# Weight tiles moved by 32 bytes, and products split at column 256 in place of 252

## The chip, the cores and the metric

The kernel runs on one core of a Trainium2 chip. The metric is the device time of the whole program in microseconds (us); smaller is better. Before the change the median of three runs is 719.89 us (717.8 to 721.41).

## What is computed

Two layers, each a linear-attention block followed by a mixture-of-experts block, on 2048 tokens of width 576, all in float32. Both layers use the same weights. Cut to what matters, one layer is:

```python
y = layernorm(x)
q, k, v = split(y @ wqkv)                      # 32 heads of 18
pq, pk = phi(q), phi(k)                        # phi(t) = where(t > 0, t + 1, exp(t)) + 1e-6
kv, z = sum_s pk^T v, sum_s pk                 # per head, over all tokens
x = x + (pq @ kv / (pq . z + 1e-6)) @ wo
y = layernorm(x)
s1, s2 = scores of y @ w_q against k1 and k2   # 32 heads, 8 + 8 sub-keys
e = argmax(s1) * 8 + argmax(s2)                # one expert of 64 for each head
x = x + sum_h gelu(y . u[e_h]) * v_expert[e_h]
```

## The kernel before, in words

**Tiling.** The 2048 tokens are 16 tiles of 128. For every tile and layer there are products with the weights: `front_k`, `front_v` and `front_q` (576 columns of output each), `back_out` (output of the attention, 576 columns), `exp_scores` (512 columns) and `exp_out` (expert results, 576 columns). In layer 1 the q products of tiles 0 to 12 are made late, by `late_q`.

**Precision.** A float32 product is made of float32r products (`F32R`): weights and tokens are each split in a high and a low part (`whi`, `wlo`; `thi`, `tlo`), and `passes` lists 14 products of 128 rows for the width of 576. `product` issues each of the 14 in two pieces, since one PSUM bank holds 512 columns: `PARTS` names for each piece its first and last column and where in the PSUM tile it goes. Each piece is one weight load on TensorE (the stationary operand, 128 x 128 of the tokens' transposed tile) and one matmul (the moving operand, 252 or 324 columns of a weight tile). A product is thus 28 matmuls, a scores product 14. `PARTS_V` places v differently: v is read back in groups of seven heads (126 columns), so its cut at 252 = 2 x 126 (`CUT`) has a reason. `row` gives the 576 columns of k, q, output and expert results as they lie in PSUM, across the boundary of two banks.

**Memory.** A pool gives out a partition's bytes in the order of declaration, each tile at a multiple of 32. As built, byte addresses within a partition and their remainders by 64:

| tile | use | before | remainder | after | remainder |
| --- | --- | --- | --- | --- | --- |
| `whi` | moving operand of k, q, v; stationary operand of `late_q` | 21,920 | 32 | 21,952 | 0 |
| `wlo`, `ohi`, `olo`, `shi`, `slo`, `vmix` | moving operands | 56,480 ... 125,600 | 32 | 56,512 ... 125,632 | 0 |
| `kvb` | plain float32 | 127,904 | 32 | 127,936 | 0 |
| `zb`, `junk`, `v5` | | 130,432 ... | 0 | 130,464 ... | 32 |
| `thif`, `tlof` and others of that pool | stationary operands | 181,504 ... | 0 | 181,536 ... | 32 |
| token tiles `x`, DMA targets and the rest of that pool | | 139,008 ... | mostly 0 | 139,040 ... | mostly 32 |

A row of `whi` is 3 x 576 x 4 = 6,912 bytes, 108 x 64, so all five blocks of a weight tile have the remainder of the tile; k and v begin 2,304 and 4,608 bytes on, multiples of 64 as well.

**Order.** On TensorE, VectorE (DVE), ScalarE (ACT) and GpSimd (POOL) the order of instructions is written out by hand (`play`, `in_order`). All DMAs are issued from SyncE's one queue (SP), in order, and SP is not among the engines whose order is fixed: there the framework's scheduler orders the issues. Some tiles are transposed by TensorE (`transposed`), others by `moved`: DVE transposes 32 x 32 blocks (`rf`, `rb`, `ro`), one DMA stores the result to DRAM (`y_df`, `y_db`, `y_do`), and four gather it back (`gf`, `gb`, `go`), after which ACT and DVE split it in `thi` and `tlo`. Names ending in f, b and o are of front, experts and output.

Of the kernel before, what the change touches and what calls it, by code (L numbers as in the profile page):

```python
# [11 lines left out]
F32 = mybir.dt.float32  # L12
# [9 lines left out]
S, D, H, DH = 2048, 576, 32, 18  # L22
P = 128
# [4 lines left out]
CUT = 2 * HC  # L28
# [36 lines left out]
def network(ctx, tc, x_in, wqkv, wo, wq_t, k_t, u_t, v2, c_mask, c_mask4, c_ident, c_code, c_code1, c_scale, c_shift, out):  # L65
    nc = tc.nc

    cp = ctx.enter_context(tc.tile_pool(name="cp", bufs=1))
# [8 lines left out]
        return t.rearrange("p (b c) -> p b c", b=2)[:, :, :HALF]  # L77

    def row(t):
        return t[:, 512 - CUT:512 - CUT + D]  # L80

    PARTS = (0, CUT, 512 - CUT), (CUT, D, 512)
    PARTS_V = (0, CUT, 0), (CUT, D, 512)


# [9 lines left out]
    nc.gpsimd.memset(mhalf, -0.5)  # L95
    kpad = cp.tile([P, 2, 56], F32, name="kpad")
    kraw = cp.tile([P, 2, E], F32, name="kraw")

    whi = cp.tile([P, NB, 3 * D], F32R, name="whi")
    wlo = cp.tile([P, 4, 3 * D], F32R, name="wlo")  # L100
# [151 lines left out]

    def product(tt, hi, lo, cols, n, parts=PARTS, rem=REM):

        o = psum(f"pp{n}")
        todo = passes(rem)
        for i, (a, b, w) in enumerate(todo):
            wb = hi[:, b] if w == "hi" else lo[:, blocks(rem)[b][1]]
            for c0, c1, at in parts:
                nc.tensor.matmul(o[:, at:at + c1 - c0], tt[a == "lo"][:, b, :], wb[:, cols + c0:cols + c1],  # L260
                                 start=(i == 0), stop=(i == len(todo) - 1))
        return o

    def pair_product(t0, t1, cols, n, parts=PARTS):

        o = [psum(f"pp{n}0_{t}") for t in (0, 1)]
        todo = sorted(passes(REM), key=lambda p: p[1])
        for i, (a, b, w) in enumerate(todo):
            wb = whi[:, b] if w == "hi" else wlo[:, blocks(REM)[b][1]]
            for p, tt in zip(o, (t0, t1)):  # L270
                for c0, c1, at in parts:
                    nc.tensor.matmul(p[:, at:at + c1 - c0], tt[a == "lo"][:, b, :], wb[:, cols + c0:cols + c1],  # L272
                                     start=(i == 0), stop=(i == len(todo) - 1))
        return o

    def phi(p, n):
        e = wk.tile([P, D], F32, tag="e", name=f"e{n}", bufs=4)
        nc.scalar.activation(e, row(p), AF.Exp)  # L278
        nc.vector.tensor_scalar(e, e, 1.0, EPS, op0=ALU.min, op1=ALU.add)  # L279
        nc.vector.scalar_tensor_tensor(e, row(p), 0.0, e, op0=ALU.max, op1=ALU.add)  # L280
        return e

    def phi_scalar(p, n):

        e = wk.tile([P, D], F32, tag="e", name=f"e{n}", bufs=4)
        nc.scalar.activation(e, row(p), AF.Relu, scale=-1.0)
        nc.scalar.activation(row(p), row(p), AF.Relu)
        nc.scalar.activation(e, e, AF.Exp, scale=-1.0)
        nc.vector.scalar_tensor_tensor(e, e, EPS, row(p), op0=ALU.add, op1=ALU.add)  # L289
        return e  # L290
# [18 lines left out]

    def front_pair(f, cols, parts=PARTS):  # L310
        pairs[f, 0, 0], pairs[f, 0, 1] = pair_product(tt["f", 0, 0], tt["f", 0, 1], cols, f, parts)
# [166 lines left out]
    def back_out(l, t):  # L478
# [4 lines left out]
        for i, (a, b, w, r) in enumerate(todo):  # L483
            for c0, c1, at in PARTS:
                nc.tensor.matmul(p[:, at:at + c1 - c0], hl[a][:r, b], w[:r, c0:c1], start=(i == 0), stop=(i == len(todo) - 1))  # L485
# [107 lines left out]
    def exp_base(l, t):  # L593

        p = tt["base", l, t] = psum(f"po{l}_{t}")
        x1 = xs.pop(("b", l, t))
        for c0, c1, at in PARTS:
            nc.tensor.matmul(p[:, at:at + c1 - c0], ident, x1[:, c0:c1], start=True, stop=False)

    def exp_out(l, t):  # L600
# [6 lines left out]
        for i in range(2):  # L607
            for c0, c1, at in PARTS:
                nc.tensor.matmul(p[:, at:at + c1 - c0], c[i], vmix[:, c0:c1], start=(i == 0 and not based), stop=(i == 1))  # L609
# [358 lines left out]
```

## Time and profile before

| | |
| --- | --- |
| median of the runs | 719.89 us |
| lowest and highest | 717.8 and 721.41 us |
| span of the profiled execution, first to last instruction | 717.5 us |
| mean granted TensorE clock | 0.996 |
| TensorE busy with matmuls | 699.1 us (97%) |
| VectorE busy | 469.5 us (65%) |
| ScalarE busy | 321.8 us (45%) |
| GpSimd busy | 202.6 us (28%) |

The profiled execution's own device time is not listed apart from its span. In the profile PE is TensorE's matmuls and PEld its weight loads. Matmuls are pipelined: the duration of one is longer than the time until the next one starts, so the rate of a stream is read from the difference of two starts. A timeline row has a group's start, the time from its first start to its last end, engine, line, operation, written tile <- read tiles, the shape of the first of them, and the count. Where an f32 matmul is not float32r (`F32`), one operation stands in the trace as two records.

### The profile page before, as it was taken

How to read it: one execution, taken by the hardware profiler on the slowest of the kernel's cores; microseconds unless marked ns; L12 is line 12 of the kernel's file. 1: busy time of each engine (PE TensorE's matmuls, PEld its weight loads, DVE VectorE, ACT ScalarE, POOL GpSimd, SP SyncE). 2: the span in 40 equal slices, each digit the busy share in tenths (PEclk: the TensorE clock that was granted, in tenths of full speed). 3: DMA queues.
4: the chain of work that ended last, by engine and by line, in shares of the span. 5: the costliest groups of instructions: out<-in, count | busy, mean ns of one | idle time of the engine just before them, and what ended most of it. 6: DMA issues, size and time to landing. Idle time of an engine off the chain costs nothing.

```text
span 717.5 us, 14670 instructions
## 1 busy us (share of the span) xinstructions
PE 699.1 (97%) x5464; PEld 650.5 (91%) x5464; DVE 469.5 (65%) x1005; ACT 321.8 (45%) x658; POOL 202.6 (28%) x544
## 2 busy tenths in 40 slices
PE   8999999999999999999999999999999999999995
PEld 5999989999998899899898989999899999999984
DVE  5533352435436877688777878552647788987986
ACT  4522332243224556455555655644543534444442
POOL 2210000111004533334344433210324244434441
PEclk9999999999999999999999999999999999999998
DMA  9947878775302322566777665513632324121101
GB/s 267 286 162 242 275 226 264 252 191 175 108 1 56 111 94 94 165 215 215 229 225 225 217 204 171 170 47 104 171 104 79 119 73 134 50 67 34 67 17 66
DMA packets 82711, 107.17 MB, mean 149 GB/s; under 512 B 8976, under 2 KB 47376, under 8 KB 82640
## 3 DMA queue, kind: packets, MB, share of 16 engines
q1 hardware_dynamic: 82640, 106.24, 47.4%
q8 instruction: 43, 0.70, 0.4%
q14 instruction: 28, 0.23, 0.1%
HBM read 68.88 MB, written 37.32 MB: 148 GB/s over the span
## 4 chain that ended last, share of the span: by engine, by line
PE 85%; DVE 5%; ACT 3%; DMA 3%; issue 2%; POOL 1%; SPq 0%; DVEq 0%; ACTq 0%; POOLq 0%
PE ppq L260 15%; PE ppo L485 15%; PE ppk L260 13%; PE ppv L260 12%; PE pps L527 10%; PE kva L527 4%; PE kva L362 2%; PE fold_ps L641 2%; PE ptb L217 2%; PE po L609 2%; DMA go<-y_do 2%; PE pto L217 2%; PE m L416 1%; PE ppk L272 1%; PE ppq L272 1%
## 5 line engine op out<-in xcount | busy, mean ns | idle before, releaser
L485 PE MATMUL ppo<-ohi,thio 126*128 126x252 f32 (+1 forms) x320 | 50.6, 300 | 4.5 <-ACT thio L119 4.4
L485 PEld LDWEIGHTS ppo<-ohi,thio 126*128 126x128 f32 (+1 forms) x320 | 44.9, 189 | 6.2 <-ACT thio L119 5.3
L260 PE MATMUL ppk<-whi,thif 128*128 128x252 f32 (+1 forms) x300 | 45.3, 298 | 0.8 <-ACT thif L119 0.8
L455 POOL TENSOR_TENSOR o<-pq,zb 128x576 f32<-128x576 f32 x19 | 27.4, 1443 | 62.5 <-ACT zb L401 58.7
L190 ACT ACTIVATE junk<-x,mb 128x576 bf16<-128x576 f32 x32 | 24.8, 775 | 44.6 <-POOL mb L189 44.4
L181 POOL TENSOR_SCALAR rsf<-mvf 128x1 f32<-128x1 f32 x16 | 3.4, 213 | 146.5 <-DVE mvf L178 146.4
L260 PE MATMUL ppv<-whi,thif 128*128 128x252 f32 (+1 forms) x300 | 44.6, 295 | 0.1
L260 PEld LDWEIGHTS ppk<-whi,thif 128*128 128x128 f32 x300 | 40.9, 188 | 4.0 <-issue 2.9
L207 ACT ACTIVATE yb<-x,rsb 128x640 f32<-128x640 f32 x32 | 29.5, 921 | 32.9 <-POOL rsb L197 32.9
L260 PE MATMUL ppv<-whi,tlof 128*128 128x252 f32 (+1 forms) x300 | 43.9, 293 | 0.0
L260 PE MATMUL ppk<-whi,tlof 128*128 128x252 f32 (+1 forms) x300 | 43.9, 293 | 0.0
L260 PEld LDWEIGHTS ppv<-whi,thif 128*128 128x128 f32 x300 | 41.3, 188 | 1.0 <-issue 0.4
L260 PEld LDWEIGHTS ppk<-whi,tlof 128*128 128x128 f32 x300 | 41.2, 188 | 0.0
L260 PEld LDWEIGHTS ppv<-whi,tlof 128*128 128x128 f32 x300 | 41.2, 188 | 0.0
L485 PE MATMUL ppo<-olo,thio 126*128 126x252 f32 (+1 forms) x256 | 39.5, 293 | 0.0
L260 PE MATMUL ppq<-whi 128*128 128x252 f32 (+1 forms) x260 | 39.5, 298 | 0.0
L485 PE MATMUL ppo<-ohi,tloo 126*128 126x252 f32 (+1 forms) x256 | 39.5, 293 | 0.0
L279 DVE TENSOR_SCALAR ek<-ek 128x576 f32<-128x576 f32 x16 | 7.3, 457 | 46.4 <-ACT ek L278 46.3
L260 PEld LDWEIGHTS ppq<-whi 128*128 128x128 f32 x260 | 36.0, 188 | 0.6 <-DVE eq L289 0.3
L485 PEld LDWEIGHTS ppo<-olo,thio 126*128 126x128 f32 x256 | 36.2, 188 | 0.0
L260 PE MATMUL ppk<-wlo,thif 128*128 128x252 f32 x240 | 36.1, 293 | 0.0
L260 PE MATMUL ppv<-wlo,thif 128*128 128x252 f32 x240 | 36.1, 293 | 0.0
(211 smaller groups left out, 1778.9 us busy)
## 6 DMA issues: line engine op xcount, KB each, us to landing
fold<-in_wq_t SPq DMA_DIRECT2D x64, 288.0 KB
whi<-hl_d SPq DMA_DIRECT2D x26, 320.0 KB
y_df<-rf SPq DMA_DIRECT2D x23, 320.0 KB
gf<-y_df SPq DMA_DIRECT2D x92, 80.0 KB
pq_d<-eq SPq DMA_DIRECT2D x19, 288.0 KB
pq<-pq_d SPq DMA_DIRECT2D x19, 288.0 KB
xf<-in_x SPq DMA_DIRECT2D x16, 288.0 KB
x<-in_x SPq DMA_DIRECT2D x16, 288.0 KB
```

What stands on the lines that cost most here:

```text
L190: nc.scalar.activation(junk, xt, AF.Square, bias=m[:, 0:1], accum_out=m[:, 1:2])
L207: nc.scalar.activation(y, x2, AF.Identity, scale=rs[:, 0:1], bias=rs[:, 1:2])
L217: nc.tensor.transpose(pt[:, b * P:(b + 1) * P], x, ident)
L260: nc.tensor.matmul(o[:, at:at + c1 - c0], tt[a == "lo"][:, b, :], wb[:, cols + c0:cols + c1], start=(i == 0), stop=(i == len(todo) - 1))
L272: nc.tensor.matmul(p[:, at:at + c1 - c0], tt[a == "lo"][:, b, :], wb[:, cols + c0:cols + c1], start=(i == 0), stop=(i == len(todo) - 1))
L279: nc.vector.tensor_scalar(e, e, 1.0, EPS, op0=ALU.min, op1=ALU.add)
L362: nc.tensor.matmul(a[64 * h:64 * h + 64, c * 72:c * 72 + n], vt[:, 2 * c + h], fk[:, f0:f0 + n], start=(t == 0 and c == 0), stop=(t == NT ...
L455: nc.gpsimd.tensor_tensor(o[:, :D], pq, zb, op=ALU.mult)
L485: nc.tensor.matmul(p[:, at:at + c1 - c0], hl[a][:r, b], w[:r, c0:c1], start=(i == 0), stop=(i == len(todo) - 1))
L527: nc.tensor.matmul(p[:, :512], hl[a == "lo"][:, b, :], shi[:, b] if w == "hi" else slo[:, blocks(REM)[b][1]], start=(i == 0), stop=(i == l ...
L609: nc.tensor.matmul(p[:, at:at + c1 - c0], c[i], vmix[:, c0:c1], start=(i == 0 and not based), stop=(i == 1))
L641: nc.tensor.matmul(p[32 * j:32 * j + 32, at:at + c1 - c0], kpad[:, ch // 2, 24 - 8 * a:56 - 8 * a], st[:, c0:c1], start=(a == 0), stop=(a ...
```

## The change

A tile `gap` of 32 bytes is declared ahead of `whi` and filled once by GpSimd, so that everything declared behind it moves up by 32 bytes. The two pieces of k, q, output and expert results become 256 and 320 columns in place of 252 and 324; they lie in PSUM at columns 256 and 512 of the tile, in place of 260 and 512. v keeps its cut at 252, the scores their single piece of 512.

```diff
     def row(t):
-        return t[:, 512 - CUT:512 - CUT + D]
-
-    PARTS = (0, CUT, 512 - CUT), (CUT, D, 512)
+        return t[:, 256:256 + D]
+
+    PARTS = (0, 256, 256), (256, D, 512)
     PARTS_V = (0, CUT, 0), (CUT, D, 512)
...
     kraw = cp.tile([P, 2, E], F32, name="kraw")
+    gap = cp.tile([P, 8], F32, name="gap")
+    nc.gpsimd.memset(gap, 0.0)
 
     whi = cp.tile([P, NB, 3 * D], F32R, name="whi")
```

TensorE, VectorE and ScalarE have the same instructions in the same order as before, GpSimd the one fill more. The scheduler orders SP's issues anew, though. Line numbers behind the gap are higher by two. The stretch of SP's queue around the gathers of tile 11 in the steady part of layer 0, before the change (`y_db0_11` is stored, its four gathers `gb0_11` follow, then `y_df1_9`, stored for tile 9 of layer 1, and its gathers):

```order
L233 DMA y_db0_11_5245<-rb0_11_5243 128x640
L617 DMA x_d9_147<-x20_9_5249 128x576
L239 DMA gb0_11_5349<-y_db0_11_5245 32x4x160 x4
L233 DMA y_df1_9_5358<-rf1_9_5356 128x640
L239 DMA gf1_9_5385<-y_df1_9_5358 32x4x160 x4
```

And after it:

```order
L235 DMA y_db0_11_5247<-rb0_11_5245 128x640
L619 DMA x_d9_149<-x20_9_5251 128x576
L235 DMA y_df1_9_5360<-rf1_9_5358 128x640
L241 DMA gb0_11_5351<-y_db0_11_5247 32x4x160 x4
L241 DMA gf1_9_5387<-y_df1_9_5360 32x4x160 x4
```

The store of `y_df1_9` went ahead of the four gathers of `gb0_11`; the same happens at tiles 7, 9 and 13. Earlier in the queue, near the end of layer 0's front, before the change:

```order
L707 DMA vst_2114<-in_v 64x576
L708 DMA vst_2114<-in_v 64x576
L712 DMA ust_2117<-in_u_t 128x64 x2
L714 DMA ust_2117<-in_u_t 64x64
L715 DMA ust_2117<-in_u_t 64x64
L712 DMA ust_2117<-in_u_t 128x64
L677 DMA xf_15_2088<-in_x 128x576
L233 DMA y_df0_11_1959<-rf0_11_1957 128x640
```

And after it:

```order
L679 DMA xf_15_2090<-in_x 128x576
L235 DMA y_df0_11_1961<-rf0_11_1959 128x640
L709 DMA vst_2116<-in_v 64x576
L710 DMA vst_2116<-in_v 64x576
L241 DMA gf0_11_2077<-y_df0_11_1961 32x4x160 x4
L714 DMA ust_2119<-in_u_t 128x64 x2
```

Here the load of token tile 15 and the store and gathers of tile 11 went ahead of the loads for the experts (`vst`, `ust`).

## The prediction

> **What bounds the kernel now.** I read the page's shares first, then the table by stage (windows), then the chain of waits, and last the timeline of TensorE. The page's first and fourth parts:
>
> ```profile
> PE 699.1 (97%) x5464; PEld 650.5 (91%) x5464; DVE 469.5 (65%) x1005; ACT 321.8 (45%) x658; POOL 202.6 (28%) x544
> ...
> PE 85%; DVE 5%; ACT 3%; DMA 3%; issue 2%; POOL 1%; SPq 0%; DVEq 0%; ACTq 0%; POOLq 0%
> ```
>
> A busy PE row need not be a PE at its peak, so the stages decide. Columns: window, its length, busy time of PE, weight loads, DVE, ACT, POOL, granted clock, DMA share, GB/s.
>
> ```profile
> 30.00:210.00 180.00, 180.00 (x1691) 169.69 (x1690) 73.77 (x148) 54.44 (x126) 13.58 (x39) 1.00 0.63 198
> 300.00:440.00 140.00, 134.90 (x1038) 126.94 (x1037) 114.23 (x244) 79.78 (x166) 54.90 (x145) 1.00 0.67 211
> 560.00:640.00 80.00, 79.98 (x547) 75.17 (x546) 68.65 (x154) 35.97 (x70) 33.74 (x93) 1.00 0.28 89
> 640.00:700.00 60.00, 59.98 (x393) 55.06 (x391) 53.06 (x126) 30.16 (x58) 24.28 (x67) 1.00 0.12 40
> ```
>
> From 30 to 210 us PE never stops and nothing else comes near it: a nanosecond off a matmul there is one off the span. Between 300 and 440 us PE loses 5 us to waits, and from 560 us on DVE is 86 to 88% busy, so a faster PE would soon wait for it. The granted clock is 1.00 throughout: nothing is to be had from the clock.
>
> How fast does the matmul stream run? The timeline merges neighbours, and the difference of two starts is the time of the group between them. Here are one `k` product, and one scores product between two others:
>
> ```profile
> 331.13 1.46 PE L260 MATMUL ppk<-whi,thif 128*128 128x252 f32 x10
> 332.43 1.20 PE L260 MATMUL ppk<-wlo,thif 128*128 128x252 f32 x8
> 333.47 1.46 PE L260 MATMUL ppk<-whi,tlof 128*128 128x252 f32 x10
> 334.77 1.50 PE L485 MATMUL ppo<-ohi,thio 126*128 126x252 f32 x10
> ...
> 339.74 1.10 PE L527 MATMUL kva<-slo,thib 128*128 128x512 f32 x4
> 340.67 1.33 PE L527 MATMUL kva<-shi,tlob 128*128 128x512 f32 x5
> ```
>
> Ten matmuls, five pairs of 252 + 324 columns, take 332.43 - 331.13 = 1.30 us: 260 ns a pair, 0.451 ns a column. The scores take 0.93 / 4 = 232.5 ns for 512 columns, 0.454 ns. What could a column cost? The durations of single matmuls by shape:
>
> ```profile
> L260 PE MATMUL ppk<-whi,tlof 128*128 128x324 f32 x150 | 40.5, 308 | 0.0
> L260 PE MATMUL ppk<-whi,tlof 128*128 128x252 f32 x150 | 39.5, 278 | 0.0
> L598 PE MATMUL po<-x,ident 128*128 128x324 f32 x6 | 2.1, 436 | 0.0
> L598 PE MATMUL po<-x,ident 128*128 128x252 f32 x6 | 1.8, 375 | 0.0
> ```
>
> 72 columns more cost 308 - 278 = 30 ns, 0.417 ns each. The plain-float32 matmul of L598 streams at half this rate (two cycles a column): 61 ns for 72 columns, 0.42 ns a cycle. So 576 columns could be streamed in about 576 x 0.42 = 242 ns, and 512 in 215; the kernel takes 260 and 232.5. **About 7% of the float32r stream is lost at something periodic**: 18 ns in 576 columns are 43 cycles, some 36 of which are 1 in 16 columns, that is, one for every 64 bytes.
>
> **The change, part by part.** As built, `whi` starts at byte 21,920 of a partition, which is 32 past a multiple of 64, and every weight tile behind it has the same remainder; the second piece starts 1,008 bytes on, at remainder 16. No float32r moving operand starts at a multiple of 64 today. Afterwards `whi` is at 21,952 (remainder 0) and a piece at 1,024 bytes on as well: all moving operands of k, q, output, scores and expert results are at 0. Of v only the first piece is; its second stays at remainder 48.
>
> *Moving operands.* The trace has no aligned float32r stream, so the price is bounded: nothing, if the lost cycle belongs to reading 4 bytes a cycle wherever one starts, and the whole loss if it comes from 64-byte reads that straddle two 64-byte rows. What the whole loss is worth: k, q and output make 32 products each of 14 pairs, expert results 64 pairs, together 1,408 pairs x 18 ns = 25.3 us. Of v, 448 pairs gain on the first piece alone, 18 x 252/576 = 8 ns: 3.6 us. Scores: 448 x (232.5 - 215) = 7.8 us. **Together 36.7 us.** I take the upper end as the likelier, because alignment at this grain is visible in one place, the next term. The columns stay 576 in both splits, so 256 + 320 in itself costs and saves nothing.
>
> *Stationary operands.* The gap of 32 bytes pushes everything behind the weights too, and `kvb` (2,528 bytes, 39.5 x 64) flips the remainder once more: the transposed tiles that are loaded as stationary operand go from remainder 0 to 32. The late q products of layer 1 take theirs out of `whi`, at remainder 32, today. Pieces of the chain, start and length in us:
>
> ```profile
> 42.91 3.64 PE ppq L260 x28
> ...
> 541.50 3.69 PE ppq L260 x28
> ```
>
> The first is a layer-0 product (stationary at 0), the second a late one (at 32): 0.05 us more for 28 matmuls. If this is due to the remainder, 115 products go over to it: 115 x 0.05 = 5.8 us; the 13 late ones get 0.65 back. Bounds 0 and 6; I take 5 with the gain, since both fit one cause.
>
> *SP's queue.* PE, DVE, ACT and POOL keep their order, and POOL gets one fill of 128x8 as one of its first instructions, while the first input is still on its way; it hides there, and uncovered would cost at most what a larger one does:
>
> ```profile
> 337.42 0.16 POOL L530 MEMSET s<- 128x64 f32 x1
> ```
>
> SP's order is set by a scheduler and changes: four times (gb of tiles 7, 9, 11, 13) the store `y_df` goes ahead of four gathers `gb` that stood before it. Timeline, tile 11:
>
> ```profile
> 395.93 2.59 SPq L239 DMA_DIRECT2D gb<-y_db  x4
> 399.32 0.34 SPq L233 DMA_DIRECT2D y_df<-rf  x1
> 401.51 1.76 SPq L239 DMA_DIRECT2D gf<-y_df  x4
> ...
> 398.45 0.83 DVE L231 STREAM_TRANSPOSE rf<-yf 128x640 f32<-128x640 f32 x1
> ...
> 402.00 0.73 ACT L119 ACTIVATE thib<-gb 128x640 fp32r<-128x640 f32 x1
> ...
> 403.84 1.42 PE L527 MATMUL kva<-shi,thib 128*128 128x512 f32 x5
> ```
>
> The store waits for `rf`, ready at 399.28; the gathers then leave at 399.7 instead of 395.93, 3.8 us later, the last at about 401.8. The store leaves at 399.32 and the first gather that reads it at 401.51, so a transfer lands some 2.2 us after its issue: the split `thib` starts near 404.0 instead of 402.00, ends at 404.7, and scores that began at 403.84 wait 0.9 us. Tiles 7, 9 and 13 by the same reckoning:
>
> ```profile
> 331.92 1.74 SPq L239 DMA_DIRECT2D gb<-y_db  x4
> 333.95 0.34 SPq L233 DMA_DIRECT2D y_df<-rf  x1
> ...
> 336.65 0.73 ACT L119 ACTIVATE thib<-gb 128x640 fp32r<-128x640 f32 x1
> ...
> 338.49 1.41 PE L527 MATMUL kva<-shi,thib 128*128 128x512 f32 x5
> ...
> 365.22 1.75 SPq L239 DMA_DIRECT2D gb<-y_db  x4
> 367.06 0.38 SPq L233 DMA_DIRECT2D y_df<-rf  x1
> 369.45 0.73 ACT L119 ACTIVATE thib<-gb 128x640 fp32r<-128x640 f32 x1
> 371.29 0.95 PE L527 MATMUL kva<-shi,thib 128*128 128x512 f32 x3
> ...
> 428.55 2.49 SPq L239 DMA_DIRECT2D gb<-y_db  x4
> 431.92 0.34 SPq L233 DMA_DIRECT2D y_df<-rf  x1
> ```
>
> Their gathers leave at 334.3, 367.5 and 432.3: 2.4, 2.3 and 3.7 us later. Tile 7 then lands near 337.8 and its scores wait about 0.15 us; tile 9 near 370.9, and they wait 0.4; tile 13 has some 2 us to spare. All four: 0.9 + 0.4 + 0.15, say 1.5 us. Bounds: 0, and the sum of the delays, 12.2 us. The loads of `ust` slip too, by up to 10 us near 150 us, and have time:
>
> ```profile
> 211.24 0.45 ACT L731 ACTIVATE shi<-ust 128x320 fp32r<-128x320 f32 x1
> ```
>
> *What is given back.* In the windows from 300 to 440 and 560 to 700 us, 280 of 717 us, PE is near other limits. If PE work falls 5%, DVE's 88% there becomes 93%, and the gathers between 300 and 440 us do not get faster. Least is lost if everything on the chain that is PE (85%, of 97% that PE is busy) follows: 12%, 4.4 us; most if those windows follow by nothing, 280/717 or 39%, 14.3 us. I take a quarter, 9 us.
>
> **Sum** against the profiled span: 36.7 - 9 - 5 - 1.5 = 21 us; 717.5 - 21 = 696.5. The median of the runs, 719.89, lies 2.4 us above the span, so **699 us**.
>
> **Rivals.**
>
> *A: the loss is in the rate, not in the address.* For it: 252 columns at remainder 32 and 324 at remainder 16 lose the same per column, and the L598 rows, with the 252 at remainder 0 and the 324 at 48, give 0.42 ns a cycle across both, so at half rate the address is nothing. Also the change moves moving and stationary operands together: they stay 32 bytes apart as before, and if only their distance counts, nothing happens. Against it: the late q rows. Then SP's 1.5 us remain: 721 us, 717 to 723. The Trainium skill, page "SBUF — State Buffer", section "Specifications (TRN2)", speaks for this rival: it gives lines of 16 bytes, with a penalty at each crossing to a new one; remainders 32 and 16 start on such a line already, so by that rule nothing is gained. The trace here fits as well a grain of 64.
>
> *B: slower.* The moving stream gains nothing, but the stationary loads at remainder 32 now cost in 115 products what they cost in the 13 late ones: +5.8 - 0.65, and scores pay about half of a pair's 3.6 ns each, 448 x 1.8 = 0.8 us. Place: every TensorE stage; it decides as soon as the moving gain is under 7.5 us. 719.9 + 6 + 1.5 = 727 us, 724 to 729. For it speaks the only row that has a stationary operand at 32; against it, that these also lie in the weight tile itself, so the cause may be another.
>
> *C: half.* Only the piece that starts on its tile's own boundary gains, or DVE takes back half: 36.7/2 - 6.5 = 12 us: 708 us, 705 to 714.
>
> For the floor, the Trainium skill, page "TensorE: Matmul & The Clock Gate", section "Back-to-back issue gap", gives N/2.4 + 2.5 ns: 245 ns a pair by estimate, against 260 measured; the sum by it would be some 4 us smaller. The sum above goes by the rows.
>
> **How the numbers follow.** Forecast 0.44 (691 to 705 by itself: 4.4 us given back and half the stationary price, 28 us; 15 us given back and all of it, 15 us), C 0.07, A 0.28, B 0.21. A measurement of this kernel tells about 0.5% from no change: 716.3 to 723.5. Faster: forecast and C, 0.51. Same: nearly all of A, 0.27. Slower: B and A's tail, 0.22. The range has to hold both signs: from 691, below which a sixth of the forecast's chance lies, to 726, above which half of B lies: 691 to 726.
>
> **What would show it.** Right: products of x28 near 3.45 us in the chain for k, q and output, v near 3.53, scores under 222 ns; PE's busy time down by 25 us or more, and more idle time of PE ahead of the scores and output between 300 and 440 us. Rival A: x28 still at 3.64 and late q too. Rival B: 3.69 everywhere, except the late q at 3.64. The SP step is wrong if `thib<-gb` waits for no DMA longer than now. The forecast falls with the first product between 30 and 210 us: there is nothing else that could shorten that stage.

## The result

The changed kernel takes 724.23 us (median of four runs, 723.09 to 724.62) against 718.85 us of the kernel before beside it. The ratio is 1.0074, with a 95% interval of 1.0045 to 1.0103: slower by 5.4 us, where 699 us was forecast. The profiled execution has a span of 722.7 us (717.5 before), at a mean granted clock of 0.996 as before.

The page of the changed kernel, its first and fourth parts:

```profile
PE 704.2 (97%) x5464; PEld 655.0 (91%) x5464; DVE 467.3 (65%) x1005; ACT 321.7 (45%) x658; POOL 201.9 (28%) x545
...
PE 73%; DVE 8%; DMA 6%; ACT 5%; issue 3%; SPq 3%; POOL 2%; DVEq 0%; ACTq 0%; POOLq 0%
```

PE is busy 5.1 us longer with the same 5464 matmuls over the same columns. The chain goes less over PE (73%, 85% before) and more over SP's queue, DMA and DVE: somewhere a wait has come in that was not there. The table by stage of the changed kernel says where (window, its length, busy time of PE, weight loads, DVE, ACT, POOL, granted clock, DMA share, GB/s):

```profile
30.00:210.00 180.00, 178.05 (x1664) 167.74 (x1663) 71.38 (x141) 53.70 (x125) 13.51 (x39) 1.00 0.63 200
300.00:440.00 140.00, 136.76 (x1049) 128.82 (x1049) 114.03 (x245) 78.16 (x163) 54.45 (x144) 1.00 0.69 213
```

Between 30 and 210 us, where PE never stopped before, it now stops for 1.95 us, and gets through 27 matmuls fewer (1664 in place of 1691). Between 300 and 440 us it waits less than before, 3.2 us in place of 5.1; 0.5 us of this is only that the last of these waits now falls behind 440 us, and up to 445 us it is 3.7 us in place of 5.1.

The streams themselves, from the timeline of the changed kernel: a piece of a `k` product and the start behind it, and a piece of a scores product and the start behind it.

```profile
337.30 1.48 PE L262 MATMUL ppk<-whi,tlof 128*128 128x256 f32 x10
338.62 1.49 PE L487 MATMUL ppo<-ohi,thio 126*128 126x256 f32 x10
...
343.85 1.10 PE L529 MATMUL kva<-slo,thib 128*128 128x512 f32 x4
344.79 1.33 PE L529 MATMUL kva<-shi,tlob 128*128 128x512 f32 x5
```

Five pairs of 256 + 320 columns take 1.32 us, 264 ns a pair, against 260 ns for 252 + 324 before. Four scores matmuls take 0.94 us, 235 ns each, against 232.5: no column has become cheaper. Whole products, from the chains: first a v product of the kernel before, then of the changed kernel a v product, a q product of layer 0 and a late q product of layer 1.

```profile
39.27 3.64 PE ppv L260 x28
...
39.32 3.64 PE ppv L262 x28
42.96 3.69 PE ppq L262 x28
...
545.89 3.73 PE ppq L262 x28
```

The v product kept its cut at 252, got an aligned first piece, and takes the 3.64 us it took before. The q product was cut anew and went from 3.64 to 3.69 us. The late q product went from 3.69 to 3.73.

### The profile page after: what moved, and what is told of

Its sections match the earlier page's. It is cut to its first block, busy times and chain, and to the rows that moved or that the text cites. A ratio compares the mean times of both kernels' runs of the same rounds, so it can differ in the third digit from the quotient of the medians.

```text
span 722.7 us, 14663 instructions
## 1 busy us (share of the span) xinstructions
PE 704.2 (97%) x5464; PEld 655.0 (91%) x5464; DVE 467.3 (65%) x1005; ACT 321.7 (45%) x658; POOL 201.9 (28%) x545
## 4 chain that ended last, share of the span: by engine, by line
PE 73%; DVE 8%; DMA 6%; ACT 5%; issue 3%; SPq 3%; POOL 2%; DVEq 0%; ACTq 0%; POOLq 0%
PE ppq L262 14%; PE ppo L487 13%; PE ppk L262 11%; PE ppv L262 10%; PE pps L529 10%; PE ptb L219 2%; PE fold_ps L643 2%; PE kva L364 2%; PE kva L529 2%; PE po L611 2%; SPq L241 2%; PE pto L219 2%; PE m L418 1%; DMA y_df<-rf 1%; DMA go<-y_do 1%
## 5 line engine op out<-in xcount | busy, mean ns | idle before, releaser
L487 PE MATMUL ppo<-ohi,thio 126*128 126x256 f32 (+1 forms) x320 | 50.6, 300 | 2.9 <-ACT thio L121 2.9
L262 PE MATMUL ppk<-whi,thif 128*128 128x256 f32 (+1 forms) x300 | 45.9, 299 | 0.8 <-ACT thif L121 0.8
L262 PE MATMUL ppk<-whi,tlof 128*128 128x256 f32 (+1 forms) x300 | 44.3, 294 | 0.0
L487 PE MATMUL ppo<-olo,thio 126*128 126x256 f32 (+1 forms) x256 | 40.1, 295 | 0.0
L487 PE MATMUL ppo<-ohi,tloo 126*128 126x256 f32 (+1 forms) x256 | 40.0, 295 | 0.0
L262 PE MATMUL ppq<-whi 128*128 128x256 f32 (+1 forms) x260 | 39.9, 300 | 0.0
L487 PEld LDWEIGHTS ppo<-olo,thio 126*128 126x128 f32 x256 | 36.7, 189 | 0.0
L487 PEld LDWEIGHTS ppo<-ohi,tloo 126*128 126x128 f32 x256 | 36.5, 189 | 0.0
L262 PE MATMUL ppk<-wlo,thif 128*128 128x256 f32 x240 | 36.5, 294 | 0.0
```

## The experiments

Two theories stood at the start. **Theory 1: the split costs.** The address of the moving operand is worth nothing, and 256 + 320 columns take longer than 252 + 324; what SyncE's new order adds is small. **Theory 2: the addresses cost**, be it the stationary operand at remainder 32 (rival B of the prediction) or another effect of the gap, which hides a gain of the moving operand. Later a third question came in: what SyncE's order costs by itself.

The runs that were timed against the kernel before, which took 718 to 719 us beside them:

| kernel | pieces | gap | order of SyncE | median, us | ratio, 95% interval | profiled span, us |
| --- | --- | --- | --- | --- | --- | --- |
| the change | 256 + 320 | yes | new | 724.23 | 1.0074, 1.0045 to 1.0103 | 722.7 |
| gap alone | 252 + 324 | yes | as before | 718.31 | 0.9991, 0.9977 to 1.0004 | 717.3 |
| split alone | 256 + 320 | no | new | 724.64 | 1.0084, 1.0064 to 1.0104 | 722.9 |
| order alone | 252 + 324 | no | new | 721.35 | 1.0040, 1.0023 to 1.0057 | 718.3 |
| change, old order | 256 + 320 | yes | as before | 722.47 | 1.0058, 1.0043 to 1.0073 | 720.7 |
| distance 96 | 252 + 324 | no | as before | 724.37 | 1.0081, 1.0059 to 1.0103 | 722.0 |
| scores at distance 0 | 252 + 324 | no | as before | 717.15 | 0.9986, 0.9971 to 1.0002 | 715.8 |
| split at 248 | 248 + 328 | no | as before | 722.29 | 1.0053, 1.0033 to 1.0072 | 721.0 |

### Streams of TensorE alone, by address and by size

A kernel of its own in place of the network: float32r matmuls one behind the other, 56 for each case, with start addresses and piece sizes chosen.

```diff
+    def group(name, pieces, mv, st, n=28, where=None, step=1728):
+        p = ps.tile([P, 1024], F32, tag="ps", name=name)
+        t = high if where is None else where
+        for i in range(n):
+            b = i % NB
+            w = t[:, st + b * P:st + b * P + P]
+            for c0, c, at in pieces:
+                m = low[:, mv + b * step + c0:mv + b * step + c0 + c]
+                nc.tensor.matmul(p[:, at:at + c], w, m, start=(i == 0), stop=(i == n - 1))
```

> No network here: TensorE alone streams groups of 28 pairs of float32r matmuls, with the split, the start addresses of both operands, the place in PSUM and the place of the stationary operand varied, and nothing else running; the output is a copy of the input. Theory now (the sizes of the two pieces decide, addresses do nothing): 252 + 324 takes 260 ns a pair at every start address, 256 + 320 about 264 at every start address, wherever the pieces go in PSUM. Rival (start addresses decide): the pairs change by 3 ns or more between moving operand at remainder 32 and 0 with one split. Rival (stationary address): they change between stationary at 0 and 32. If the stationary operand's place next to the moving one is what the late q products pay for, the two groups with it there take 3 ns more a pair than the same split with it far off. If the loss is 1 in 16 columns whatever the sizes, all other splits take 260 as well.

Measured, from the timeline of this kernel. The names say the split (`old` 252 + 324, `new` 256 + 320), and the remainder of moving (`mv`) and stationary (`st`) operand in units of 16 bytes (`two` is 32); `stlow` has its stationary operand in the moving operand's own tile, both at the same remainder.

```profile
23.11 7.45 PE L42 MATMUL oldxmvtwoxstzero<-low,high 128*128 128x252 f32 x56
30.40 7.54 PE L42 MATMUL oldxmvzeroxstzero<-low,high 128*128 128x252 f32 x56
37.78 7.63 PE L42 MATMUL oldxmvzeroxsttwo<-low,high 128*128 128x252 f32 x56
45.25 7.46 PE L42 MATMUL oldxmvbothxaligned<-low,high 128*128 128x252 f32 x56
52.55 7.50 PE L42 MATMUL newxmvtwoxstzero<-low,high 128*128 128x256 f32 x56
59.89 7.63 PE L42 MATMUL newxmvzeroxstzero<-low,high 128*128 128x256 f32 x56
67.35 7.67 PE L42 MATMUL newxmvzeroxsttwo<-low,high 128*128 128x256 f32 x56
...
96.93 7.55 PE L42 MATMUL oldxstlow<-low 128*128 128x252 f32 x56
104.31 7.62 PE L42 MATMUL newxstlow<-low 128*128 128x256 f32 x56
```

Two neighbouring starts divided by 28 give a pair, with the change from one case to the next in it: (30.40 - 23.11) / 28 = 260.4 ns for the split and the remainders of the kernel before, (37.78 - 30.40) / 28 = 263.6 with the moving operand moved to remainder 0. Within a case, without its first and last pairs, the values are 260.0 and 263.5 ns. The aligned stream is the slower one, and the expectation of one rate at every address has failed. With the stationary operand moved to 32 instead, the pair takes (45.25 - 37.78) / 28 = 266.8 ns. With both pieces started at a multiple of 64 it is 260.2: aligning gains nothing in any form. For 256 + 320 they are 262.4 (moving at 32, stationary at 0), 266.8 (both at 0) and 268.2 (moving at 0, stationary at 32). The split costs 2.4 ns a pair at the old remainders. Where in PSUM the pieces lie makes 1 ns or less.

The last two rows answer the late q products. Their 3.69 us do not come from a remainder of 32, but from the two operands being at the same remainder: 263.6 ns for 252 + 324. So what counts looks like the distance of the two, as rival A of the prediction had said in passing.

### The gap alone

```diff
     kraw = cp.tile([P, 2, E], F32, name="kraw")
+    gap = cp.tile([P, 8], F32, name="gap")
+    nc.gpsimd.memset(gap, 0.0)
```

> The 32 bytes alone, split kept at 252; SP's order is that of before. Sizes decide: ratio 1.000 (within 0.003), k products of 28 matmuls at 3.64 us. Addresses decide: about 1.007 as with the whole change.

Measured: ratio 0.9991 (0.9977 to 1.0004), no difference. The chain of this kernel, a q and a late q product:

```profile
42.77 3.64 PE ppq L262 x28
...
541.44 3.70 PE ppq L262 x28
```

They are the rows of before. Here the first pieces of k, q, output and expert results and all scores start at remainder 0 (the second pieces, 1,008 bytes on, at 48) and all stationary tiles at 32: the addresses of the change, without its sizes, are worth nothing in either direction. A gain of the moving operand hidden by a loss of the stationary one would show in the late q product, whose two operands both came from 32 to 0; it stayed at 3.70 us. Theory 2 falls, and with it the forecast's moving term and rival B's stationary one.

### The split alone

```diff
-        return t[:, 512 - CUT:512 - CUT + D]
-
-    PARTS = (0, CUT, 512 - CUT), (CUT, D, 512)
+        return t[:, 256:256 + D]
+
+    PARTS = (0, 256, 256), (256, D, 512)
```

> The split at 256 alone, no gap; SP's order is that of the whole change. Sizes decide (or SP's new order): ratio 1.007, k products of 28 matmuls near 3.69 us. Addresses decide: 1.000 and 3.64 us.

Measured: 1.0084 (1.0064 to 1.0104), span 722.9 us: the whole loss of the change, without the gap. Both pieces start at remainder 32 here and at 0 in the change, and the time is the same: this is the test of full alignment at these sizes, and it too finds nothing. The order of SyncE's issues is the changed kernel's too. So it is the sizes of the matmuls, not the addresses, that made the scheduler order the loads anew.

The trace of this run has one thing that the others lack (a stretch with its granted clock, third number from the end, and two rows of its timeline):

```profile
176.00:179.00 3.00, 3.00 (x23) 2.93 (x21) 1.63 (x4) 0.00 (x0) 0.92 (x3) 0.50 0.79 238
...
176.63 2.73 PE L260 MATMUL ppk<-whi,thif 128*128 128x256 f32 x10
179.18 1.22 PE L260 MATMUL ppk<-wlo,thif 128*128 128x256 f32 x8
```

The granted clock is 0.50 from 176 to 179 us, right behind a wait of TensorE of 2.03 us, and the ten `ppk` matmuls take 2.55 us in place of the changed kernel's 1.42. In the changed kernel, with a wait as long (1.95 us), the clock stayed at 1.00 there, so it is not shown that the wait brings this on; in this execution it made the loss over 1 us larger.

### What counts of an address

The distance of the moving operand's start from the stationary one's, in steps of 8 bytes, again in streams alone:

```diff
+    for r in range(0, 32, 2):                 # 4 bytes each: distance 0, 8, 16 ... 120
+        group("old" + L[r], split(252), r, 0, 20)
+    for r in range(0, 32, 2):
+        group("full" + L[r], [(0, 512, 0)], r, 0, 24)
...
+    group("oldstat", split(252), 0, 24, 20)
+    group("oldfar", split(252), 8 + 32, 0, 20)
+    group("oldfarther", split(252), 8 + 64, 0, 20)
```

> Streams alone again, 20 pairs each, nothing else running, the output a copy of the input. Now the stationary operand stays at a multiple of 128 bytes and the moving operand's start goes from 0 to 124 bytes past one, for 252 + 324, 248 + 328, 256 + 320, 288 + 288 and 512 columns. Theory (what counts is the distance between the two starts, modulo 128, together with the sizes): 252 + 324 takes 260 ns at distance 32, 263.5 at 0; the group with the stationary operand at 96 and the moving one at 0 (distance 32) takes 260 too, and so do those 128 and 256 bytes further; 512 columns take 233 at 32 and 227 at 0. Rival (the distance counts modulo 64): distance 96 takes 260 like 32. If some distance brings a pair under 257 ns, there is a version faster than both kernels; if the rate only steps between 260 and 267, the kernel before stands at the best point already.

Measured, 252 + 324 at distances 0, 8, 16, 24, 32 and 40 bytes (20 pairs each; timeline of this kernel):

```profile
23.09 5.45 PE L42 MATMUL olda<-low,high 128*128 128x252 f32 x40
28.38 5.58 PE L42 MATMUL oldc<-low,high 128*128 128x252 f32 x40
33.80 5.36 PE L42 MATMUL olde<-low,high 128*128 128x252 f32 x40
39.00 5.49 PE L42 MATMUL oldg<-low,high 128*128 128x252 f32 x40
44.33 5.37 PE L42 MATMUL oldi<-low,high 128*128 128x252 f32 x40
49.54 5.56 PE L42 MATMUL oldk<-low,high 128*128 128x252 f32 x40
```

Starts apart by 5.29, 5.42, 5.20, 5.33 and 5.21 us; within a case 263.9, 272.0, 260.0, 266.8, 259.9 and 270.1 ns a pair. Moving the stationary operand by 96 in place of the moving one by 32 gives 260.3, and distances of 160 and 288 bytes give 260.0: the distance counts modulo 128. The distance alone does not settle every value, though: 96 gave 264.5 ns here, by the moving operand, and 266.8 above, by the stationary one. The whole sweep for 252 + 324 runs from 259.9 to 272.0. The distances that are multiples of 16 average 263.3, those between them 268.6. The Trainium skill, page "SBUF — State Buffer", section "Specifications (TRN2)", has lines of 16 bytes with a penalty at each crossing to a new one. The sweep agrees with that grain, at some 5 ns a pair, and the kernel is on it before and after.

The kernel before, at distance 32, stands at the lowest of the sampled values. 256 + 320 is at 262.2 there and at 263.4 to 267.1 elsewhere, 248 + 328 at 260.2. So the old cut sits on a good point by its size, too, and both tiles move by 32 together in the change, which leaves the distance where it was.

### The distance changed in the kernel

`kpad` (448 bytes) is declared behind the weights in place of ahead of them, which puts the moving operands at distance 96; the sizes stay 252 + 324.

```diff
-    kpad = cp.tile([P, 2, 56], F32, name="kpad")
     kraw = cp.tile([P, 2, E], F32, name="kraw")
...
     vmix = cp.tile([P, D], F32R, name="vmix")
+    kpad = cp.tile([P, 2, 56], F32, name="kpad")
```

> Split at 252, SP's order of before; the tile kpad (64 bytes modulo 128) is declared behind the weights, so that every weight tile starts 96 bytes past a multiple of 128 and the transposed tiles stay at 0. Theory (the distance between the two starts modulo 128 counts): 264.5 ns a pair as in the streams, 4.5 ns x 1,674 pairs = 7.5 us more, scores and late q as before: ratio 1.010, k products of 28 matmuls near 3.70 us. Rival (in the kernel only the sizes matter): 1.000 and 3.64 us.

Measured: 1.0081 (1.0059 to 1.0103). From the chain of this kernel, a q and a late q product:

```profile
42.98 3.73 PE ppq L260 x28
...
546.05 3.69 PE ppq L260 x28
```

3.73 us where the distance changed, v included, and 3.69 as ever where it did not, since moving and stationary operand of a late q product lie in one tile. That the distance counts is thereby shown in the kernel itself, for these products. The size was near: the pair takes 266.7 ns where 264.5 was expected, and summed over the trace k, v, q and output take 8.6 us more where 7.5 was expected. The run takes 6.2 us more; between 300 and 440 us TensorE waits 2.7 us in place of 5.1, which is 2.4 us of the difference.

### The scores at distance 0

The one place where the streams promised a gain: 512 columns took 227.0 ns at distance 0 and 233.4 at 32. `vmix` and `kvb` are declared ahead of the scores' weights, and the late q's stationary blocks start 96 bytes later.

```diff
+    vmix = cp.tile([P, D], F32R, name="vmix")
+    kvb = cp.tile([P, 4 * HC + P], F32, name="kvb")
     shi = cp.tile([P, NB, 512], F32R, name="shi")
     slo = cp.tile([P, 4, 512], F32R, name="slo")
...
-        at = (1 + t // 2 % 2) * D + t % 2 * 2 * P
+        at = (1 + t // 2 % 2) * D + t % 2 * 2 * P + 24
```

> The kernel before with its tiles declared in another order, so that the scores' weights start at a multiple of 128 (distance 0 from the transposed tiles, where the stream of 512 columns took 227 ns in place of 233), all other weights staying at distance 32; and the late q products read their stationary operand 96 bytes further on (distance 32 in place of 0). Theory: 448 x 6.4 ns = 2.9 us and 182 x 3.3 ns = 0.6 us less, ratio 0.995. If the gain is eaten by waits elsewhere: 0.998 to 1.000.

Measured: 0.9986 (0.9971 to 1.0002), which cannot be told from no change. All scores together take 0.7 us less (232.2 ns a matmul, 233.8 before), not the 6.4 ns each that the streams promised; the late q products fall from 263 to 260 ns a pair, 0.4 us in all. For the scores, then, the stream alone does not carry over to the kernel. No version was found that is measurably faster than the kernel before.

### Another size: 248 + 328

```diff
-    PARTS = (0, CUT, 512 - CUT), (CUT, D, 512)
+    PARTS = (0, 248, 264), (248, D, 512)
```

> k, q, output and expert results split at 248 (248 + 328 columns), nothing else; SP's order of before. Theory (each size has its own rate at a given distance): 260.2 ns a pair in the streams at distance 32, so ratio 1.000, k products at 3.64 us. Rival (any split other than 252 costs): 1.007.

Measured: 1.0053 (1.0033 to 1.0072), and 264.5 ns a pair, where the streams alone had 260.2. A miss: the stream alone does not carry over to the kernel for this size either. SyncE's order is that of before here, so not every new size changes it. Whether the place in a sequence decides was tried with products of 14 pairs behind different work:

```diff
+        for r in range(5):                      # one behind the other
+            one(who + "same" + L[r], c)
+        for r in range(5):                      # behind a v product
+            one(who + "vee" + L[r], 252, at=0)
+            one(who + "turn" + L[r], c)
+        for r in range(5):                      # behind five matmuls of 128 columns
+            group(who + "few" + L[r], [(0, 128, 0)], 8, 0, 5)
+            one(who + "small" + L[r], c)
...
```

> TensorE streams alone again (the output is a copy of the input; the network is left out), all with moving operands at remainder 32 and stationary ones at 0: products of 14 pairs of 252 + 324, 248 + 328 and 256 + 320 columns as one stream of 70 pairs, one behind the other, behind a v product (252 + 324 written from column 0), behind five matmuls of 128 columns, and behind 14 of 512. Read: ns per pair within a product. Theory (a stream settles into one of several patterns by what stood before it, and keeps it): 248 + 328 takes 260 in the long stream and 264 to 265 behind v products or small matmuls, as it did in the whole kernel; 256 + 320 takes 262 to 263 in the long stream and 263 to 265 behind others; 252 + 324 takes 260 wherever it stands. Rival (what stands before does not matter, and the other engines' traffic makes the difference in the whole kernel): the same value in all five places, 260 for 248 + 328, 262.5 for 256 + 320, within 0.5 ns.

Measured, from the timeline of this kernel: two products one behind the other, of 252 + 324 (`old`), 248 + 328 (`two`) and 256 + 320 (`new`).

```profile
41.40 3.80 PE L42 MATMUL oldsamea<-low,high 128*128 128x252 f32 x28
45.04 3.80 PE L42 MATMUL oldsameb<-low,high 128*128 128x252 f32 x28
...
169.80 3.80 PE L42 MATMUL twosamea<-low,high 128*128 128x248 f32 x28
173.44 3.80 PE L42 MATMUL twosameb<-low,high 128*128 128x248 f32 x28
...
298.66 3.85 PE L42 MATMUL newsamea<-low,high 128*128 128x256 f32 x28
302.35 3.85 PE L42 MATMUL newsameb<-low,high 128*128 128x256 f32 x28
```

3.64, 3.64 and 3.69 us a product: 260.0, 260.0 and 263.6 ns a pair. 252 + 324 and 248 + 328 are at 260.0 in every place, after at most four uneven pairs. 256 + 320 has two patterns: pairs of 266 and 261 in turn (263.3 on average) in the long stream and behind its own kind, and 265, 265, 257 (262.4) behind v products and small matmuls, kept to the end of the product; behind 14 matmuls of 512 columns it falls into either. So for 256 + 320 there are several patterns, as the theory says, but with the values the other way round: the slower one was expected behind other work. For 248 + 328 the theory fails. The latter takes 267, 263 and 264 ns in turn in the kernel, as regularly, for a cause that stays open; the rival, traffic of other engines, was not tried.

### The order of SyncE's issues alone

The kernel before, with its 498 issues on SyncE pinned in the order that the changed kernel has:

```diff
+    SP_ORDER = [
+        0, 1, 2, 3, 4, 5, 6, 7, 8, 9, 10, 11, 12, 13, 14, 15, 16, 17, 18, 19, 20, 21, 22, 23,
...
+    for x, y in zip(SP_ORDER, SP_ORDER[1:]):
+        tc.add_manual_dep(dm[y], dm[x].name, mybir.DependencyInfo(mybir.DependencyClass.NoSync, mybir.DependencyReason.DATA),
+                          reason="in_order")
```

> The kernel before, with SP's 498 issues held in the order that they have in the changed kernel. If SP's new order does the harm: ratio 1.007. My step in the prediction: 1.5 us, ratio 1.002, scores of tile 11 about 0.9 us late. Theory now (the matmul stream alone sets the time): within 0.002 of 1.000.

Measured: 1.0040 (1.0023 to 1.0057), 2.9 us: more than either 0 or the prediction's 1.5 us, and less than the whole loss. First the timeline of the kernel before around the first attention; in brackets stands what an instruction waited for:

```profile
159.87 0.38 SPq L233 DMA_DIRECT2D y_df<-rf  x1
165.09 0.85 DVE L231 STREAM_TRANSPOSE rf<-yf 128x640 f32<-128x640 f32 x1 [0.34 <-DMA y_df<-rf]
168.34 0.92 ACT L207 ACTIVATE yf<-xf,rsf 128x640 f32<-128x640 f32 x1 [3.19 <-POOL rsf L183]
170.39 0.76 DVE L280 SCALAR_TENSOR_TENSOR ek<-ppk,ek 128x576 f32<-128x576 f32 x1
171.55 1.43 PE L362 MATMUL kva<-ek,v 128*64 128x72 f32 x40
```

and the same with the new order alone:

```profile
160.81 0.38 SPq L233 DMA_DIRECT2D y_df<-rf  x1
167.03 0.85 DVE L231 STREAM_TRANSPOSE rf<-yf 128x640 f32<-128x640 f32 x1 [2.82 <-DMA y_df<-rf]
170.27 0.93 ACT L207 ACTIVATE yf<-xf,rsf 128x640 f32<-128x640 f32 x1 [5.67 <-POOL rsf L183]
172.33 0.76 DVE L280 SCALAR_TENSOR_TENSOR ek<-ppk,ek 128x576 f32<-128x576 f32 x1
173.23 1.43 PE L362 MATMUL kva<-ek,v 128*64 128x72 f32 x40 [2.16 <-DVE ek L280]
```

The loads of `ust` have moved to just ahead of those of `wob`, and the store `y_df` stands behind both in the one queue: it leaves at 160.81 in place of 159.87, takes 6.2 us to land in place of 5.2, and frees its buffer at 167.03 in place of 165.09, so DVE waits 2.82 us before it may transpose the next tile. DVE takes its instructions in the order written out for it, and so everything behind is late by 1.9 us: the statistics, POOL's `rsf`, ACT's `yf`, then ACT's and DVE's part of `ek`, for which the products `kva` of the attention wait. Nothing that reads `ust` is late. The same products in the changed kernel, and in the gap alone, which has the old order:

```profile
174.57 1.43 PE L364 MATMUL kva<-ek,v 128*64 128x72 f32 x40 [1.95 <-DVE ek L282]
...
172.44 1.43 PE L364 MATMUL kva<-ek,v 128*64 128x72 f32 x40 [0.94 <-DVE ek L282]
```

The three traces with the new order have this wait at 1.95 to 2.16 us. Of the six with the old order one has it at 0.94, the others at 0.1 us or less: the place had little to spare before the change, and of the wait some 1 to 2 us are the new order's. At the gathers `gb`, where the prediction had looked, the changed kernel shows this (tile 11):

```profile
403.69 1.89 SPq L241 DMA_DIRECT2D gb<-y_db  x4
...
407.74 0.74 ACT L121 ACTIVATE thib<-gb 128x640 fp32r<-128x640 f32 x1 [1.59 <-DMA gb<-y_db]
408.53 1.43 PE L529 MATMUL kva<-shi,thib 128*128 128x512 f32 x5 [0.37 <-ACT thib L121]
```

0.37 us in the changed kernel and 0.17 us with the order alone, for tile 11, and nothing of 0.15 us or more for the three other tiles.

### The change with the old order

The reverse: the changed kernel, with its issues on SyncE pinned in the order of before.

```diff
+    SP_ORDER = [
...
+        138, 139, 140, 141, 156, 157, 158, 159, 160, 161, 162, 155, 148, 163, 170, 171, 150, 151, 152, 153, 172, 173, 147, 174,
...
```

> The changed kernel (gap of 32 bytes and pieces of 256 and 320 columns) with SyncE's issues pinned in the order that they had before. Theory (two causes that add: the split costs TensorE some 4 us over all its products, and the new order of SyncE's issues costs one wait of 2 us for the keys of the first attention at 173 us): k, q and out pairs stay at 117 and 147 ns as in the changed kernel, the wait of TensorE at 173 us falls under 1 us, span 720 to 721, ratio 1.004 to 1.006. Rival (the order costs nothing together with the split, since a slower TensorE reaches the wait later): ratio 1.007 to 1.008 as the changed kernel. Second rival (the split costs nothing by itself and all of the difference is the order): ratio 0.999 to 1.001.

Measured: 1.0058 (1.0043 to 1.0073), span 720.7 us. The row of its timeline that counts has no wait left:

```profile
172.78 1.43 PE L364 MATMUL kva<-ek,v 128*64 128x72 f32 x40
```

The second rival falls by the interval; the first falls by this row and the span, for the interval's upper end just reaches its 1.007. By the runs, the split costs 0.58% (4.2 us) and the order 0.40% (2.9 us); their sum of 0.98% is above the 0.74 and 0.84% of the two kernels that have both, within the intervals. What comes late between 300 and 445 us waits less there: TensorE waits 5.1 us in the kernel before, and 4.15, 4.1 and 3.7 us with the order, the split, and both. So each cost alone loses about 1 us again, and both together 1.4; by this the two would cost a little more than their sum, so why they measured less stays open. The span of the order alone is only 0.8 us longer than before, its runs 2.9 us. Some of the 2 us between these is chance in the two traces: that of the order is 0.55 us ahead by the first v product (38.72 against 39.27 us; two traces with the old order differ by 0.3 us there), and gains 0.6 us in the last 6 us, where the granted clock between 711 and 714 us was 1.00, against 0.57 before. Without both the order costs 2.0 us there.

## Why the prediction was wrong

**What bounds the kernel** was read rightly in the main: TensorE's stream between 30 and 210 us, at 260 ns a pair. That "nothing else comes near it" was too strong: at 174 us the store `y_df` was so near that with the old order one trace waited 0.94 us for what follows it.

**The failed step is the moving operands**: "I take the upper end as the likelier, because alignment at this grain is visible in one place, the next term." It gave 36.7 us of gain; the gap alone measured none (0.9991), and 256 + 320 columns take as long with both pieces at remainder 0 (1.0074) as with both at 32 (1.0084). The loss above 0.417 ns a column is real, but the "1 in 16" was a number that happened to fit. The size experiments show it: 260.0 and 266.7 ns are 624 and 640 times 0.417 ns, steps of 16, and single sizes alternating between two banks take 117.7 ns for 256 columns, 133.3 for 288, and 146.7 for 320 and 324 alike, with a floor near 111.7 ns for anything from 128 to 224 columns. A loss of 1 in 16 would be smooth in size and have no floor. The v products, with one piece at remainder 32 and the other at 16 before and at 0 and 48 after, refute the forecast in the changed kernel's own trace: 3.64 us both times.

**"The columns stay 576 in both splits, so 256 + 320 in itself costs and saves nothing"** failed too, and this sentence is the one that turned the sign. It took the time to be linear in the columns. Summed from start to start over the two traces, k products take 1.4 us more, q 0.9, late q 0.5, output 1.1, and v, scores and expert results 0.4: some 4.3 us, or about 0.04 us in each of the 96 products of k, q and output. Why these sizes settle at a slower rate stays open. The trace of before had no second split at full speed to read this from, so its cost was unknown and had to be bounded, not set to nothing.

**The stationary operands** were costed at 5 us and cost nothing. The row behind it was read rightly (3.69 in place of 3.64 us for a late q product) and put down to the wrong one of two things that were different in it. Not the remainder of 32 but the shared tile, at distance 0, was the cause. Rival B's own doubt named this.

**SyncE's order** was near in size and wrong in place. Forecast were 1.5 us at the four gathers `gb`; there it cost 0.37 us at one tile. The cost came at 174 us, a wait of 1.95 us of which 1 to 2 us are the order's, by the step that was waved through: "The loads of `ust` slip too, by up to 10 us near 150 us, and have time". They have; the store `y_df` behind them in the queue has not. Only the readers of the moved loads were asked, not what is queued behind them.

**What is given back** had nothing to give back, but its mechanism was seen in reverse: a later TensorE found shorter waits between 300 and 445 us, 3.7 in place of 5.1 us.

**Of the rivals**, A had the address right ("if only their distance counts, nothing happens") and stayed at 721 us, since it took over the free split. B came nearest in time (727 us, "724 to 729"), by a mechanism that the gap alone shows to be absent: luck. That the stated range, 691 to 726 us, still holds the measured time is the same luck, as its upper part was there for B. What would have shown the forecast wrong was named rightly: "The forecast falls with the first product between 30 and 210 us".

**The account** of the 5.2 us between the two spans: 4.3 us by the streams, 1.95 us by the wait at 174 us, less 1.4 us of waits between 300 and 445 us. That makes 4.85 us; the remaining 0.35 us aren't assigned.

## What to carry to other kernels

A rate that is a few per cent under what the columns would allow is not evidence of misalignment: before one moves an address, a stream alone, at two or three addresses and sizes, tells in one run whether there can be anything to gain. What it is worth the kernel has to show: for 248 + 328 columns and for the scores the stream did not carry over. A split of the same columns in other sizes has a cost of its own, to be bounded like that of any operation that the trace doesn't show. Where a scheduler orders a queue, a load that moves is asked about twice: who reads it, and what stands behind it in the queue; and since new matmul sizes alone can change that order, it is compared even when no transfer was touched.

## What was not expected of the hardware

In streams alone, float32r matmuls, each with its weight load, keep a rate that depends on the sizes and on the distance between the two operands' starts modulo 128 bytes: 259.9 to 272.0 ns a pair for the same 252 + 324 columns, and 227.0 to 240 ns for one matmul of 512. Matmuls of 128, 192 and 224 columns all take 111.7 ns, so the smaller piece of a pair gains nothing by being smaller: 192 + 384 took 286.7 ns a pair. The Trainium skill, page "TensorE: Matmul & The Clock Gate", section "LDWEIGHTS (loading the stationary operand)", gives columns / 1.2 for a weight load, by estimate 107 ns for 128. The floor of 111.7 lies near it, but no run here shows that the weight load makes the floor; single load records last 192 ns there and overlap. 256 + 320 columns have more than one stable pattern, and which one a product falls into depends on what stood before it and is kept to its end (263.3 or 262.4 ns a pair); a stream alone doesn't always tell which one the kernel gets (260.0 against 264.5 for 248 + 328).
